# Shared operations offered to two engines, and float32 products on both halves of the accumulator

## The chip, the cores and the metric

The kernel runs on one core of a Trainium2 chip. The core has five engines that take their instructions from queues of their own, each in order: TensorE (PE) multiplies matrices and writes PSUM, VectorE (DVE) and ScalarE (ACT) read PSUM and SBUF, GpSimd (POOL) works on SBUF, and SyncE (SP) issues most of the transfers. They wait for each other by semaphores. The metric is the device time of one execution in microseconds (us), the median of several runs.

## The reference

Attention for 4 batches of 8 heads, 768 positions and 64 columns, in which a query sees only the keys of its own hash bucket (six sign bits of a projection), followed by a two-layer network (512 to 2048 to 512 columns, 3072 tokens) with a squared relu:

```python
q_bits = (np.einsum('bhsd,dk->bhsk', q, proj) > 0).astype(np.int64)
k_bits = (np.einsum('bhsd,dk->bhsk', k, proj) > 0).astype(np.int64)
...
mask = q_bucket[:, :, :, None] == k_bucket[:, :, None, :]
scores = scale * np.matmul(q, k.transpose(0, 1, 3, 2))
scores = np.where(mask, scores, -1000000000.0)
...
attn = attn / (np.sum(attn, axis=-1, keepdims=True) + 1e-09)
return np.matmul(attn, v).astype(np.float32)
...
x = np.ascontiguousarray(attn_out.transpose(0, 2, 1, 3)).reshape(B * S, H * D)
...
h = x @ w_in
r = np.maximum(h, 0.0)
g = s * (r * r) + b
return (g @ w_out).astype(np.float32)
```

## The kernel before

One head of one batch is a visit (32 of them); its 768 queries are worked in three chunks of 256, and a visit's chunk is a slot (96 slots). For every slot `weights` computes two score tiles of 128 x 768 on PE (L436, L437), takes the negated row maximum on DVE (L441), the exponential with its row sum on ACT (L442), four small instructions on DVE for the reciprocal (L446 to L449), and scales the weights on POOL (L454). `values` then transposes the weights on PE (L479), four tiles into a PSUM bank at a time, three banks in a slot; copies each bank to SBUF; and multiplies it with the values into the accumulator `av` in PSUM. Between the slots `prep` makes the next visit's operands: transposes (L318), split in a rounded and a rest part on ACT and DVE (L320, L321), the hash (L331 to L333), its comparison (L336), and transfers inside SBUF on SP's queue. Every second head, the result of two heads is split again (L532, L533) and stored to DRAM (`xd`), from where the network's steps (`moe`) load it.

From the ninth visit on (`FULL = 8`) products with the values are made from rounded parts (float32r): a copy of the transposed weights on ACT (L494), the rest on DVE (L495) and two matmuls for each tile, whose rows 0 to 63 and 64 to 127 of `av` are added at the end (L526 on ACT, L528 on DVE). In the first eight visits (batch 0) they are plain float32 matmuls (L503) with 64 output columns, all into partitions 0 to 63 of `av`. Their copies are placed by number: of the three banks of a slot the third goes to DVE (`FD = (2,)`, L487), the others to ACT (L489). The buffers of these visits are float32 tiles which are later exchanged for float32r tiles under the same tag.

The weights of the network arrive as packed 64-bit numbers and are decoded in 32 pieces (`decode`): two conversions on ACT (L274, L275), two bit operations on DVE (L276, L277), an addition on POOL (L278), a cast on ACT (L280) and a subtraction on POOL (L281). `decodes` says how many pieces are in the list by which slot, `PACE = 2` lets two loads be under way. The network's step of 256 tokens can begin once all eight heads of a batch have that chunk, and once its first pieces are decoded: first-layer matmuls L569 to L571, relu, square and scaling on ACT (L575 to L577), the rest part on POOL (L578, L579), second-layer matmuls L590 to L592, a copy on DVE (L597) and the store.

The order of all this is made by a list scheduler (`Plan`) while the kernel is built. Each step has one engine, an estimated duration, a priority and what it reads and writes. The scheduler takes the engine that is free first and gives it the ready step of lowest priority number:

```python
t = max(free.get(e, 0.0), min(ready[i] for i in lst))
...
i = min((i for i in open_[e] if ready[i] <= t + LOOK.get(e, 0.0)), key=lambda i: (self.steps[i][3], i))
```

The result is each engine's fixed order of instructions. Nothing is chosen while the kernel runs.

## Time and profile before

| what | us |
|---|---|
| median of three runs | 1095.4 |
| lowest and highest of them | 1088.42, 1095.47 |
| the profiled execution, its own time | 1091.88 |
| its span, first to last instruction | 1090.1 |
| PE busy in the span | 1062.0 |
| ACT busy | 654.4 |
| DVE busy | 612.9 |
| POOL busy | 502.1 |

The span is that of the profiled execution. In the rows of the profile an instruction is named by its line, engine and operation, with the tile written and the tiles read; a group's row ends with its count, busy time in us, mean duration in ns, and the idle time of the engine just before it with what ended it. A matmul's end is modelled and overlaps the next one's start, so that consecutive records are closer together than their durations say. The chain of waits follows the work back from the last instruction to what released it.

### The profile page before, as it was taken

The numbers are of one execution on the slowest core, as the hardware profiler recorded it, in microseconds if no ns is written. First come the engines' busy times: TensorE is split into PE (matmuls) and PEld (weight loads), VectorE is DVE, ScalarE is ACT, GpSimd is POOL, SyncE is SP. The second block draws the span as 40 slices with busy tenths as digits, with TensorE's granted clock in tenths as the row PEclk, the third lists the DMA queues.
The fourth block names the chain that finished last, engine by engine and source line by source line (L and its number), as shares of the span: only waits on it lengthen the run. The fifth ranks groups of instructions, "written<-read, shape, count | busy, mean of one in ns | idle before, by whom it ended". The sixth has DMA issues, their size and how long they took to land.

```text
span 1090.1 us, 18596 instructions
## 1 busy us (share of the span) xinstructions
PE 1062.0 (97%) x6948; PEld 942.4 (86%) x6948; DVE 612.9 (56%) x1181; ACT 654.4 (60%) x1265; POOL 502.1 (46%) x482
## 2 busy tenths in 40 slices
PE   7999888999999999999999999999999999999998
PEld 6666565898899999999999999999999998898987
DVE  5568886888666667666666766566667520000000
ACT  3567776888566666665666666656657553333332
POOL 2346776888644443444444443444444433333333
PEclk8999998999999999999999999999999999999999
DMA  3347565645322423332332243232323010101000
GB/s 80 83 134 201 160 189 141 160 118 175 80 55 62 121 74 82 94 92 65 92 104 64 74 112 84 54 115 66 83 54 118 3 56 33 58 1 59 17 23 20
DMA packets 85643, 94.14 MB, mean 86 GB/s; under 512 B 52832, under 2 KB 57952, under 8 KB 85552
## 3 DMA queue, kind: packets, MB, share of 16 engines
q1 hardware_dynamic: 80352, 75.90, 26.0%
q10 hardware_dynamic: 5200, 17.05, 5.1%
q8 instruction: 55, 0.90, 0.3%
q14 instruction: 36, 0.29, 0.1%
HBM read 48.24 MB, written 18.87 MB: 62 GB/s over the span
## 4 chain that ended last, share of the span: by engine, by line
PE 71%; issue 13%; POOL 8%; DVE 5%; ACT 2%; POOLq 0%; DVEq 0%; ACTq 0%
PE bank L479 11%; PE bank L436 6%; PE bank L437 6%; PE bank L503 5%; PE bank L569 5%; PE bank L570 5%; PE bank L571 5%; PE bank L590 5%; PE bank L511 5%; PE bank L591 5%; PE bank L592 5%; PE bank L510 4%; POOL glb L579 4%; POOL rb L578 3%; PE bank L318 2%
## 5 line engine op out<-in xcount | busy, mean ns | idle before, releaser
L454 POOL TENSOR_SCALAR eb<-eb,st 128x768 f32<-128x768 f32 x192 | 191.9, 1008 | 217.9 <-DVE st L449 175.2
L569 PE MATMUL bank<-xc,w 128*128 128x256 f32 x768 | 224.5, 292 | 0.0
L441 DVE TENSOR_REDUCE st<-bank 128x1 f32<-128x768 f32 x192 | 182.8, 954 | 73.9 <-PE bank L437 71.4
L570 PE MATMUL bank<-xc,w 128*128 128x256 f32 x768 | 217.0, 283 | 0.0
L571 PE MATMUL bank<-xc,w 128*128 128x256 f32 x768 | 216.9, 282 | 0.0
L442 ACT ACTIVATE eb<-bank,st 128x768 f32<-128x768 f32 x192 | 173.2, 903 | 43.3 <-DVE st L441 36.1
L494 ACT CAST phr<-bank 128x512 fp32r<-128x512 f32 x216 | 125.2, 583 | 123.1 <-PE bank L479 122.0
L578 POOL TENSOR_SCALAR rb<-rb,misc 128x512 f32<-128x512 f32 x96 | 74.8, 779 | 267.0 <-ACT ghb L577 255.7
L495 DVE TENSOR_TENSOR plb<-bank,phr 128x512 fp32r<-128x512 f32 x216 | 147.1, 686 | 80.2 <-ACT phr L494 77.9
L479 PE MATMUL bank<-ident,eb 128*128 128x128 f32 x1152 | 169.0, 276 | 4.4 <-POOL eb L454 2.9
L590 PE MATMUL bank<-w,ghb 128*128 128x512 f32 x384 | 156.5, 407 | 0.0
L592 PE MATMUL bank<-w,glb 128*128 128x512 f32 x384 | 151.4, 394 | 1.9 <-POOL glb L579 1.9
L591 PE MATMUL bank<-w,ghb 128*128 128x512 f32 x384 | 152.6, 398 | 0.0
L479 PEld LDWEIGHTS bank<-ident,eb 128*128 128x128 f32 x1152 | 135.8, 142 | 17.8 <-POOL eb L454 4.8
L569 PEld LDWEIGHTS bank<-xc,w 128*128 128x128 f32 x768 | 146.0, 190 | 4.3 <-issue 0.4
L570 PEld LDWEIGHTS bank<-xc,w 128*128 128x128 f32 x768 | 146.2, 190 | 3.1
L575 ACT ACTIVATE rb<-bank 128x512 f32<-128x512 f32 x96 | 57.5, 598 | 148.1 <-PE bank L571 145.7
L571 PEld LDWEIGHTS bank<-xc,w 128*128 128x128 f32 x768 | 146.0, 190 | 0.0
L436 PE MATMUL bank<-ks,aq 128*128 128x384 f32 x384 | 139.7, 364 | 3.6 <-ACT eb L442 3.5
L437 PE MATMUL bank<-ks,bq 76*128 76x384 f32 x384 | 131.9, 343 | 1.5 <-DVE bq L395 1.5
L579 POOL TENSOR_TENSOR glb<-rb,ghb 128x512 fp32r<-128x512 f32 x96 | 124.2, 1293 | 6.2
L510 PE MATMUL bank<-phr,vsr 128*128 128x256 f32 x432 | 115.1, 288 | 0.0
(88 smaller groups left out, 1723.3 us busy)
## 6 DMA issues: line engine op xcount, KB each, us to landing
xd<-xsb SPq DMA_DIRECT2D x48, 256.0 KB
xc<-xd SPq DMA_DIRECT2D x48, 256.0 KB
ks<-aq SPq DMA_DIRECT2D x30, 384.0 KB
raw<-in_moe_w_in_dram ACTq DMA_DIRECT2D x16, 512.0 KB
raw<-in_moe_w_out_dram ACTq DMA_DIRECT2D x16, 512.0 KB
nat<-in_q_dram SPq DMA_DIRECT2D x32, 192.0 KB
nat<-in_k_dram SPq DMA_DIRECT2D x32, 192.0 KB
ks<-bq SPq DMA_DIRECT2D x30, 192.0 KB
```

Source lines behind the costliest of these rows:

```text
L436: nc.tensor.matmul(o, aq[:, ts], ks[:, 0, cols], start=True, stop=False)
L437: nc.tensor.matmul(o, bq[0:HR, ts], ks[0:HR, 1, cols], start=False, stop=True)
L441: dve(S, lambda a=a, sc=sc: nc.vector.tensor_reduce(nm[:, a:a + 1], sc, AX.XY, ALU.max, negate=True), bk, [nk[a]], pr, 0.95)
L442: act(S, lambda a=a, sc=sc, e=e: nc.scalar.activation(e.rearrange("p (g n) -> p g n", g=2), sc, AF.Exp, bias=nm[:, a:a + 1], accum_out=z[: ...
L454: pool(S, lambda a=a, e=e: nc.gpsimd.tensor_scalar(e, e, rz[:, a:a + 1], u[:, a:a + 1], ALU.mult, ALU.add), [("st", y, 2)], [ek], pr, 1.01)
L479: nc.tensor.transpose(out=bank[:, tb, o:o + P], in_=eb[:, es[a], kt * P:(kt + 1) * P], identity=ident)
L569: nc.tensor.matmul(hp, w[:, 0, fs], xc[:, 0, :], start=(cc == 0), stop=False)
L570: nc.tensor.matmul(hp, w[:, 1, fs], xc[:, 0, :], start=False, stop=False)
L571: nc.tensor.matmul(hp, w[:, 0, fs], xc[:, 1, :], start=False, stop=(cc == NC_ - 1))
L590: nc.tensor.matmul(o, gh[:, ts], w[:, 0], start=(f == 0), stop=False)
L591: nc.tensor.matmul(o, gh[:, ts], w[:, 1], start=False, stop=False)
L592: nc.tensor.matmul(o, gl[:, ts], w[:, 0], start=False, stop=(f == NF - 1))
```

## The change

The scheduler's steps get a list of ways, each with an engine, a duration and the code for it. A step with several ways is offered to each of its engines. An engine passes it over where another would finish it sooner, and the first that takes it keeps it:

```diff
+    def any(self, ways, r=(), w=(), pr=0.0, lag=0.0):
...
-            i = min((i for i in open_[e] if ready[i] <= t + LOOK.get(e, 0.0)), key=lambda i: (self.steps[i][3], i))
+        def best(e, t):
...
+                if len(ways) > 1:
+                    mine = max(t, ready[i]) + next(c for x, c, _ in ways if x == e)
+                    if any(max(free.get(x, 0.0), ready[i]) + c < mine - 1e-9 for x, c, _ in ways if x != e):
+                        continue
...
+    def some(n, fn, r, w, pr, ways):
+        cost = {ACT: 0.095 + n / 1050.0, DVE: (n + 64) / 960.0 + 0.05, POOL: 0.15 + n / 760.0}
+        eng = {ACT: nc.scalar, DVE: nc.vector, POOL: nc.gpsimd}
+        plan.any([(e, cost[e], lambda e=e: fn(eng[e])) for e in ways], r, w, pr)
```

Offered to ACT and DVE are the copies of the transposed weights, the first half of the accumulator's copy, the relu and the output copy; to ACT and POOL the casts of decoded weights and of `xsb`. All of these copies are one line of the changed kernel, L197. The subtraction for `xsb` goes from DVE to POOL in all cases:

```diff
-                if f in FD:
-                    dve(512, lambda: nc.vector.tensor_copy(ph(), src), [("b", tb)], [("ph", y)], pr, 0.65)
-                else:
-                    act(512, lambda: nc.scalar.copy(ph(), src), [("b", tb)], [("ph", y)], pr)
+                copy(512, lambda: ph, lambda: src, [("b", tb)], [("pf", y)], pr, (ACT, DVE))
...
-        act(CH, lambda: nc.scalar.copy(xh, av[0:D]), [("b", 4)], xk, pr)
-        if w >= FULL:
-            dve(CH, lambda: nc.vector.tensor_tensor(xh, xh, av[D:P], ALU.add), [("b", 4)], xk, pr, 0.42)
+        copy(CH, lambda: xh, lambda: av[0:D], [("b", 4)], xk, pr, (ACT, DVE))
+        dve(CH, lambda: nc.vector.tensor_tensor(xh, xh, av[D:P], ALU.add), [("b", 4)], xk, pr, 0.42)
...
-            act(CH, lambda: nc.scalar.copy(xsb[:, 0, :], t), xk, [("xs", 0)], pr)
-            dve(CH, lambda: nc.vector.tensor_tensor(xsb[:, 1, :], t, f32(xsb[:, 0, :]), ALU.subtract), xk + [("xs", 0)], [("xs", 1)], pr, 0.5)
+            copy(CH, lambda: xsb[:, 0, :], lambda: t, xk, [("xs", 0)], pr, (ACT, POOL))
+            pool(CH, lambda: nc.gpsimd.tensor_tensor(xsb[:, 1, :], t, f32(xsb[:, 0, :]), ALU.subtract), xk + [("xs", 0)], [("xs", 1)], pr)
...
-        act(512, lambda: nc.scalar.copy(wt[key][:, 0], g), [gk], [key + (0,)], pr)
+        copy(512, lambda: wt[key][:, 0], lambda: g, [gk], [key + (0,)], pr, (ACT, POOL))
...
-            act(2 * CH, lambda r=r: nc.scalar.activation(r, bank[:, 5, :], AF.Relu), [("b", 5)], [rk], MP)
+            some(2 * CH, lambda e, r=r: e.activation(r, bank[:, 5, :], AF.Relu) if e is nc.scalar else e.tensor_scalar(r, bank[:, 5, :], 0.0, None, ALU.max), [("b", 5)], [rk], MP, (ACT, DVE))
```

The float32 products of the first eight visits alternate. The two tiles of a bank are m = 0 and 1; the first goes to partitions 0 to 63 of `av` and the second to 64 to 127, and the two halves are added at the end as in the later visits. The planner's duration for a pair goes from 0.87 to 0.62 (`FPC`):

```diff
-                        nc.tensor.matmul(av[0:D], VS[x][:, 0, kt], PH[y][:, m], start=(kt == 0), stop=(kt == NT - 1))
-                pe(0.87, mm, [("ph", y)] + vk, [("b", 4)], pr)
+                        nc.tensor.matmul(av[m * D:(m + 1) * D], VF[x][:, kt], PF[y][:, m], start=(f == 0), stop=(f == HT - 1))
+                pe(FPC, mm, [("pf", y), ("vf", x)], [("b", 4)], pr)
```

Their buffers `VF` and `PF` (four in place of three) lie where the last four decoded pieces come later, so that those four loads wait for the eighth visit's end (`held`); the float32r tiles exist from the start. The first two visits' preparation (`prep_still`) works in two halves of 384 columns with transposes of q and k together, half of its key casts are on DVE, and in the new order all of the second visit's preparation stands on DVE ahead of the first reduction. One broadcast transfer to `ks` becomes two. The four small instructions stay on DVE (`SMALL = "dve"`), and `SPLIT = ()` leaves its branches unused. The numbers of the planner change:

```diff
-        return min(ND, int(FIRST * max(0, i - EARLY // 3)) if i < EARLY else 8 + int(RATE * (i - EARLY)))
+        n = int(FIRST * max(0, i - DSTART)) if i < EARLY else int(FIRST * (EARLY - DSTART)) + int(RATE * (i - EARLY))
+        return min(n, ND if i >= H * NCH else ND - 4)
...
-FIRST = 1.2
-RATE = 4.0
+FIRST = 0.8
+RATE = 6.0
 PACE = 2
+DSTART = 3
...
-RATE_DMA = 1.9e5
+RATE_DMA = 2.2e5
...
-FD = (2,)
+FPC = 0.62
```

Three places show what this does to the order. The first is PE near the end of the second visit. `nat` are the next visit's inputs, `eb` the weights that are transposed, `pf` their copies, `vf` the values; the number after a row is how often it stands there in a row. Before:

```order
L503 MATMUL bank<-pf_77,vf_75 64x256 x2
L503 MATMUL bank<-pf_78,vf_75 64x256 x2
L318 MATMUL bank<-ident,nat_66 128x128 x3
L479 MATMUL bank<-ident,eb 128x128 x8
L503 MATMUL bank<-pf_79,vf_75 64x256 x2
L331 MATMUL bank<-aq_68,pjh 64x384
L332 MATMUL bank<-aq_68,pjl 64x384
L333 MATMUL bank<-bq_70,pjh 64x384
L479 MATMUL bank<-ident,eb 128x128 x4
```

And now:

```order
L535 MATMUL bank<-pf_79,vf_76 64x256 x4
L374 MATMUL bank<-aq_68,pjh 64x384
L375 MATMUL bank<-aq_68,pjl 64x384
L376 MATMUL bank<-bq_70,pjh 64x384
L520 MATMUL bank<-ident,eb 128x128 x8
L535 MATMUL bank<-pf_78,vf_76 64x256 x2
L520 MATMUL bank<-ident,eb 128x128 x8
L535 MATMUL bank<-pf_78,vf_76 64x256 x2
L535 MATMUL bank<-pf_79,vf_76 64x256 x4
```

Transposes of two and three banks stand together now, and the products of two banks follow each other; of 144 matmuls before and after, the stretches of one, two and three banks were 26, 11 and 8 and are 27, 12 and 7.

The second is DVE around the first decoded piece (`raw`, `osb`), in the ninth slot. `st` are row statistics, `xpb` the result of two heads, `xsb` its split. Before:

```order
L441 TENSOR_REDUCE st<-bank 128x1
L487 COPY pf_79<-bank 128x512
L533 TENSOR_TENSOR xsb<-xpb,xsb 128x256
L336 TENSOR_SCALAR nat_66<-bank,misc 44x384
L441 TENSOR_REDUCE st<-bank 128x1
L487 COPY pf_79<-bank 128x512
L446 TENSOR_SCALAR st<-st 128x2
L447 TENSOR_SCALAR st<-st 128x2
L448 RECIPROCAL st<-st 128x2
L449 SCALAR_TENSOR_TENSOR st<-st 128x2
L276 TENSOR_SCALAR raw_194<-osb 128x512
L277 SCALAR_TENSOR_TENSOR osb<-osb,raw_194 128x512
```

And now:

```order
L197 COPY pf_78<-bank 128x512
L470 TENSOR_REDUCE st<-bank 128x1
L197 COPY xpb<-bank 64x256
L363 SCALAR_TENSOR_TENSOR bq_70<-bank,misc,aq_68 128x384
L559 TENSOR_TENSOR xpb<-xpb,bank 64x256
L487 TENSOR_SCALAR st<-st 128x2
L488 TENSOR_SCALAR st<-st 128x2
L489 RECIPROCAL st<-st 128x2
L490 SCALAR_TENSOR_TENSOR st<-st 128x2
L318 TENSOR_SCALAR raw_196<-osb 128x512
L379 TENSOR_SCALAR nat_66<-bank,misc 44x384
L319 SCALAR_TENSOR_TENSOR osb<-osb,raw_196 128x512
```

The subtraction for `xsb` has left, the copy of the accumulator's first half (L197, `xpb`) and the addition of its second half (L559) have come.

The third is POOL at the first pieces. `eb` is the scaling of the weights, `w` a decoded weight. Before:

```order
L454 TENSOR_SCALAR eb<-eb,st 128x768 x4
L278 TENSOR_TENSOR osb<-osb,raw_196 128x512
L454 TENSOR_SCALAR eb<-eb,st 128x768 x2
L281 TENSOR_TENSOR w_857<-osb,w_857 128x512
L278 TENSOR_TENSOR osb<-osb,raw_193 128x512
L281 TENSOR_TENSOR w_893<-osb,w_893 128x512
```

And now:

```order
L495 TENSOR_SCALAR eb<-eb,st 128x768 x2
L320 TENSOR_TENSOR osb<-osb,raw_196 128x512
L197 CAST w_688<-osb 128x512
L564 TENSOR_TENSOR xsb<-xpb,xsb 128x256
L323 TENSOR_TENSOR w_688<-osb,w_688 128x512
L320 TENSOR_TENSOR osb<-osb,raw_197 128x512
L495 TENSOR_SCALAR eb<-eb,st 128x768 x2
```

Between the scalings stand now the weight cast that was ACT's and the `xsb` subtraction that was DVE's.

More of the change, by code (lines that the diff above doesn't have):

```diff
@@ L407, in prep_values @@
+        return [lambda i, pr, f=f, g=g: f(g, i, pr) for f in (split, hash_) for g in range(2)]
     def prep_values(w, pr):
@@ L425, in weights @@
         aq, bq, ks = AQ[x], BQ[x], KS[x]
-        nm, z, rz, u = [st[:, y, m] for m in range(4)]
+        nm, z, rz, u, fl = [st[:, y, m] for m in range(5)]
         nk, zk = [[("st", y, m, a) for a in range(TPC)] for m in range(2)]
@@ L470, in tiles @@
         def tiles(f):
-            tb, y = fill_bank(i), nfill[1] % NPH
-            nfill[1] += 1
+            tb, full = fill_bank(i), w < FULL and f not in SPLIT
+            y = nfill[2] % 4 if full else nfill[1] % NPH
+            nfill[2 if full else 1] += 1
             src = bank[:, tb, :]
```

232 lines of the change are left out of this document (127 added, 105 removed).

## The prediction

> **What bounds the kernel now.** I read the page first: the busy shares and the slices of the span.
>
> ```profile
> span 1090.1 us, 18596 instructions
> PE 1062.0 (97%) x6948; PEld 942.4 (86%) x6948; DVE 612.9 (56%) x1181; ACT 654.4 (60%) x1265; POOL 502.1 (46%) x482
> PE   7999888999999999999999999999999999999998
> DVE  5568886888666667666666766566667520000000
> ```
>
> TensorE (PE) is busy for 97% of the span. DVE comes near it only in the first quarter, and that is where PE shows its 8s. So I cut the span into stages and read the windows view: to the last transposes of the third slot (a slot is one head and 256 query rows), to those of the 24th slot, which ends the first batch's attention, then to the 36th, to the end of attention, and to the end. The columns are the length, then the busy time of PE, weight loads, DVE, ACT and POOL, the granted clock, and the DMA share and rate.
>
> ```profile
> core 0: us, PE busy (x) PEld busy (x) DVE busy (x) ACT busy (x) POOL busy (x), PEclk, DMA share, GB/s
> 0.00:41.30 41.30, 34.82 (x174) 26.38 (x175) 23.64 (x64) 16.71 (x31) 11.76 (x18) 0.92 0.21 55
> 41.30:195.60 154.30, 141.90 (x759) 96.98 (x757) 117.35 (x222) 112.55 (x230) 91.88 (x79) 0.98 0.60 166
> 195.60:328.30 132.70, 130.74 (x894) 120.74 (x893) 102.08 (x172) 98.58 (x192) 93.02 (x83) 1.00 0.42 115
> 328.30:880.00 551.70, 549.99 (x3837) 515.49 (x3836) 358.70 (x705) 351.77 (x702) 232.64 (x234) 1.00 0.30 80
> 880.00:1090.10 210.10, 204.55 (x1293) 182.85 (x1291) 11.12 (x19) 74.78 (x112) 72.84 (x71) 1.00 0.10 33
> ```
>
> From 195.6 us on PE is busy for 98.5% and then 99.7% of its stage, so nothing that other engines do there can give much. The second stage is the place: 154.3 us for 21 slots, PE busy 141.9 (92%), DVE 117.4 (76%), ACT 112.6 (73%), POOL 91.9 (60%). The chain of waits and the groups of that stage say what PE does there.
>
> ```profile
> by line: PE bank L503 30.3%; PE bank L479 14.8%; PE bank L436 8.4%; PE bank L437 7.2%; issue 5.8%; DVE st L449 3.1%; DVE st L441 3.0%; PE bank L318 3.0%; DVE raw L276 2.6%; POOL eb L454 2.5%; PE bank L331 2.3%; ACT pf L489 2.2%; DVE pf L487
> L503 PE MATMUL bank<-pf,vf 128*64 128x256 f32 x252 | 64.2, 392 | 5.3 <-ACT pf L489 3.9 <-DVE pf L487 1.2
> ```
>
> The float32 products of the first eight heads (L503) hold 30.3% of the chain and 64.2 of PE's 141.9 us. Most of the rest of the chain is PE too. So in this stage PE is the bound, and these products are its largest item.
>
> **The products.** Before, every product adds into partitions 0 to 63 of the accumulator. The trace has 288 records for the 144 matmuls of the order: each float32 matmul runs as two.
>
> ```profile
> 100.27 1.08 PE L503 MATMUL bank<-pf,vf 128*64 128x256 f32 x4
> 105.85 1.94 PE L503 MATMUL bank<-pf,vf 128*64 128x256 f32 x8
> 45.34 2.80 PE L503 MATMUL bank<-pf,vf 128*64 128x256 f32 x12
> ```
>
> Four records (one pair of products) take 1.08 us, eight 1.94, twelve 2.80: 0.215 us for each record more, and 0.22 for each stretch. After the change the two products of a pair go to partitions 0 to 63 and 64 to 127. If the halves run side by side while records of one half follow each other in order, a stretch of n pairs takes 2n+1 steps of 0.215 where it took 4n: the first record alone, the last alone, each second record of one half beside the first of the other. Over the whole order the changed kernel has 27 stretches of one pair, 12 of two and 7 of three, and saves (27x1 + 12x3 + 7x5) x 0.215 = 98 x 0.215 = 21.1 us of PE, 252/288 of it, 18.4, in the second stage and 2.6 in the first. No trace shows two halves at once, so the bounds are 0 (the row as it is) and 31 (144 steps gone, if no step stood alone); a loss is left out, since the records stay as many and as long. I take 21, since the two records of a matmul are seen in order in the row and nothing in the program ties one half to the other.
>
> The Trainium skill, "TensorEngine Tiling (Array Packing)", section "Key Properties", says that column tiles operate independently, and "TensorE: Matmul & The Clock Gate", Part 3, gives three column tiles a measured 2.38x. By an estimate from that figure (79% of the ideal, so 1.59x for two halves) 62 us of steps would become 39 and the saving would be 23. No run here shows it.
>
> **What the scheduler moves.** With 18.4 less, PE would be busy 123.5 us in the stage, and then DVE is the question. Its rows there, with two of the whole span for work that is new to it:
>
> ```profile
> L441 DVE TENSOR_REDUCE st<-bank 128x1 f32<-128x768 f32 x41 | 38.7, 952 | 16.5 <-PE bank L437 16.3
> L277 DVE SCALAR_TENSOR_TENSOR osb<-osb,raw 128x512 int32<-128x512 int32 x19 | 17.4, 921 | 0.3
> L487 DVE COPY pf<-bank 128x512 f32<-128x512 f32 x21 | 14.4, 685 | 6.2 <-PE bank L479 6.1
> L276 DVE TENSOR_SCALAR raw<-osb 128x512 int32<-128x512 int32 x19 | 11.8, 629 | 0.0
> L449 DVE SCALAR_TENSOR_TENSOR st<-st 128x2 f32<-128x2 f32 x21 | 9.1, 432 | 0.8
> L533 DVE TENSOR_TENSOR xsb<-xpb,xsb 128x256 fp32r<-128x256 f32 x11 | 7.9, 715 | 0.6 <-ACT xsb L532 0.6
> L528 DVE TENSOR_TENSOR xpb<-xpb,bank 64x256 f32<-64x256 f32 x72 | 30.5, 424 | 47.0 <-ACT xpb L526 45.5
> L489 ACT COPY pf<-bank 128x512 f32<-128x512 f32 x42 | 23.8, 585 | 9.2 <-PE bank L479 8.9
> L280 ACT CAST w<-osb 128x512 fp32r<-128x512 f32 x19 | 11.8, 619 | 4.6 <-POOL osb L278 4.4
> L526 ACT COPY xpb<-bank 64x256 f32<-64x256 f32 x21 | 7.6, 363 | 10.2 <-PE bank L503 10.1
> L418 POOL TENSOR_TENSOR vsr<-vn,vsr 128x384 fp32r<-128x384 f32 x24 | 25.3, 1054 | 43.8 <-ACT vsr L417 43.6
> L578 POOL TENSOR_SCALAR rb<-rb,misc 128x512 f32<-128x512 f32 x96 | 74.8, 779 | 267.0 <-ACT ghb L577 255.7 <-PE bank L437 10.9
> ```
>
> I counted the rows of both orders between the sixth and the 48th reduction (slots 4 to 24). On DVE: 22 more additions of the two halves (new L559, priced by L528: 22 x 0.424 = 9.3), 7 more copies of transposed weights (x 0.685 = 4.8), 8 copies of the sum (priced like L528, 3.4), two more decode pairs that come earlier (2 x (0.921 + 0.629) = 3.1), and 10 subtractions for xsb gone to POOL (10 x 0.715 = -7.2). That is +13.4: 130.8 us. ACT loses 8 copies of 0.585, 8 of 0.363, 10 weight casts of 0.619 and a few small ones, 14 us in all: 99. POOL gains 11 subtractions of 256 columns and 11 casts of 512 and 4 of 256. Its own rows bound the two-input kind by 1.05 (L418, 384 columns) from above and the casts by 0.78 (L578, 512 columns); I take 0.8, 0.8 and 0.5, about 20 us: 112. DVE has become the busiest engine, at 131 where PE stood at 142.
>
> The length of the stage is the busy time of its busiest engine over the share that this engine reaches. PE reaches 92% now. DVE reached 95% and 97% in two slices in which it had work waiting:
>
> ```profile
> 120.00:130.00 10.00, 7.93 (x43) 5.13 (x42) 9.47 (x19) 8.38 (x17) 5.53 (x6) 1.00 0.58 170
> 130.00:140.00 10.00, 10.00 (x54) 6.93 (x53) 9.71 (x16) 7.33 (x15) 7.61 (x7) 1.00 0.40 112
> ```
>
> Over the whole stage it has only 76%, waiting for PE most. I take 90%, just under the 92% of today's busiest engine, because DVE's work comes in pieces that wait for three engines: 131/0.90 = 145.5 us, 8.8 less than 154.3. The ends are 100% (131, so -23) and today's 76% (172, so +18).
>
> **The rest.** First stage: the products save 2.6 there. The order now puts all of the second head's preparation on DVE ahead of the first reduction. Before, part of it came later:
>
> ```profile
> 20.70 1.07 DVE L393 TENSOR_SCALAR ks<-bank,misc 12x768 fp32r<-12x768 f32 x1 [1.73 <-PE bank L391]
> 21.78 1.07 DVE L395 TENSOR_SCALAR bq<-bank,misc 12x768 fp32r<-12x768 f32 x1
> ```
>
> So the first softmax starts later and the next two don't stop for these 2.1 us. One half of the key casts moves to DVE as well. I take -1, between -2.6 and +4. The broadcast to ks becomes two transfers, 30 more issues on SP; the preparation of a head runs a whole head (some 22 us) ahead, which hides an issue; without that cover PE's scores would wait for it. Later stages: 11 of 96 relus go to DVE, 18 of 22 output copies to ACT, hidden under a PE that is 98 to 99.7% busy with both engines near 65% of it; 0, within 3 either way. The last four decodes now wait for the buffers of the first eight heads; the order has them at slots 29.5 to 31 (32nd decode before: 32.5), so 0.
>
> **Sum.** -8.8 - 1 + 0 = -9.8 on the profiled execution's 1091.88 us: 1082 us. That execution lies 3.5 us under the median of the three runs (1095.4) and 3.5 over the lowest.
>
> **Rivals.** (A) PE stays the bound: DVE's copies fall into its gaps, PE keeps its 92%, and the stage is 123.5/0.92 = 134. DVE would need 98% of that; with DVE at the 96% of its best slices it is 136.5. That gives -17.8 and -2.6: 1071 us. For it: DVE's idle time is mostly waiting for PE. Against it: that share was never held for long.
>
> (B) The halves don't run side by side. PE keeps 142 in the stage, DVE's 131 fits beside it, and all stays: 1092 us, up to 1097 if DVE held only 82% (131/0.82 = 160). For it: no row shows an overlap.
>
> (C) POOL holds up DVE. DVE's instructions with SBUF operands are stretched where a POOL instruction is in flight:
>
> ```profile
> 100.56 0.16 DVE L449 SCALAR_TENSOR_TENSOR st<-st 128x2 f32<-128x2 f32 x1
> 111.14 0.68 DVE L277 SCALAR_TENSOR_TENSOR osb<-osb,raw 128x512 int32<-128x512 int32 x1
> 111.90 1.30 POOL L278 TENSOR_TENSOR osb<-osb,raw 128x512 int32<-128x512 int32 x1 [1.27 <-DVE st L446]
> 112.14 1.08 DVE L449 SCALAR_TENSOR_TENSOR st<-st 128x2 f32<-128x2 f32 x1
> 113.40 2.40 POOL L454 TENSOR_SCALAR eb<-eb,st 128x768 f32<-128x768 f32 x2 [0.20 <-DVE st L449]
> 113.61 1.33 DVE L277 SCALAR_TENSOR_TENSOR osb<-osb,raw 128x512 int32<-128x512 int32 x1
> 120.90 0.42 DVE L276 TENSOR_SCALAR raw<-osb 128x512 int32<-128x512 int32 x1
> ```
>
> L277 takes 0.68 us alone and 1.33 beside L454; L449 takes 0.16 alone and 1.08 beside L278; L276 alone takes 0.42. The excess in the stage is 19 x (0.921 - 0.68) + 19 x (0.629 - 0.42) + 21 x (0.432 - 0.16) = 14.3 us with POOL busy 60% of the time. With POOL at 112/145 = 77% it grows to 18.3: DVE 135, the stage 150 at 90%, and the time 1086 us. The Trainium skill, "SBUF — State Buffer", section "Who interferes with whom", calls this an exclusive lock, held for the whole instruction; by that rule moving work to POOL speaks against this change, and the rows agree.
>
> (D) Slower: the handoffs, not the load, set DVE's share, so it stays at 76% while the load grows. Each score tile waits on PE and then on DVE:
>
> ```profile
> DVE st L441 <- PE bank L437: 16.3, 14, 2.7
> ACT eb L442 <- DVE st L441: 11.4, 18, 1.5
> ```
>
> The stage becomes 131/0.76 = 172 and the time 1091.9 + 18 - 1 = 1109 us. It turns into a loss of 1% once DVE's share stays under 79% (131/0.79 = 166). Against it: the 16.3 us that DVE waits for scores come from a PE full of products, which shrink.
>
> **Chances.** The forecast 0.42 (its own range 1075 to 1090), A 0.17, B 0.16, C 0.15, D 0.10. About 1% (11 us) is what a measurement can tell from no change here, so faster begins under 1084.4 against the median. Two thirds of the forecast's cases, all of A and a few of C lie there: 0.28 + 0.17 + 0.04 = 0.49. Slower is D alone, 0.10. The rest is 0.41. The range 1068 to 1094 leaves out the far end of A, the upper part of B and D, about 0.18.
>
> **What would show it.** The eight-record stretches of the new L535 at about 1.3 us and the twelves near 1.7, and a group of some 45 us in place of 73 would show the overlap; stretches of 1.94 show B. The last transposes of the 24th slot at 186 us and DVE's busy share near 90% in the stage confirm the middle step; a share under 80% with the same overlap is D, and PE above 90% there is A. L319 well above 0.92 is C. The forecast is wrong as a whole if the time moves after the 24th slot: PE should stay at 98% or more from there to the end of attention.

## The result, and the profile after

The changed kernel takes 1083.6 us (median of 7 runs, 1081.6 to 1085.5) where the kernel before took 1095.3 on the same chip: a ratio of 0.991, 95% interval 0.989 to 0.994. The profiled execution took 1081.91 us, 9.97 less than the 1091.88 of the one before. The seven executions of the kernel before fall into two groups, 1088.4 to 1088.6 and 1095.3 to 1095.6 us, and its profiled one lies between them, so the parts compared below, which are of one execution each, carry some us of chance.

The page of the profiled execution: span, busy time of the engines, then the slices of the span for PE, DVE and the granted clock.

```profile
span 1080.0 us, 18674 instructions
...
PE 1039.1 (96%) x6936; PEld 928.1 (86%) x6936; DVE 654.3 (61%) x1270; ACT 607.2 (56%) x1141; POOL 552.7 (51%) x557
...
PE   6979887999999999999999999999999999999998
...
DVE  6889896988777777768787677667767400000000
...
PEclk7999997999999999999999999999999999999999
```

PE is 23 us less busy than before, but the span is only 10 shorter. In three of the first seven slices PE shows a lower digit than before, DVE has risen to 8s and 9s in five of them, and the clock stands at 7 in two slices where it stood at 8. The windows view, cut at the same events as before (columns: length, busy time of PE, weight loads, DVE, ACT and POOL, granted clock, DMA share and rate):

```profile
0.00:40.10 40.10, 31.19 (x157) 23.36 (x158) 27.95 (x78) 16.81 (x33) 13.62 (x24) 0.83 0.28 65
40.10:190.70 150.60, 126.56 (x770) 84.66 (x768) 127.29 (x245) 101.38 (x202) 112.90 (x106) 0.93 0.62 173
190.70:323.40 132.70, 129.66 (x880) 119.96 (x879) 109.06 (x187) 89.42 (x169) 96.39 (x89) 0.99 0.40 111
323.40:855.30 531.90, 531.90 (x3747) 501.50 (x3746) 387.40 (x756) 316.19 (x613) 248.97 (x263) 1.00 0.31 83
855.30:1080.00 224.70, 219.76 (x1393) 198.60 (x1391) 2.63 (x6) 83.44 (x125) 80.83 (x79) 1.00 0.09 30
```

| part | before | after | difference | forecast |
|---|---|---|---|---|
| first stage | 41.3 | 40.1 | -1.2 | -1 |
| second stage | 154.3 | 150.6 | -3.7 | -8.8 |
| from the 24th slot to the end | 894.5 | 889.3 | -5.2 | 0 |

The sum is the forecast one (-10.1 for -9.8), its parts are not. In the second stage PE fell from 141.9 to 126.6 us, but its share fell from 92% to 84%; DVE, at 127.3, has 84.5%. So neither engine fills the stage. The products themselves did more than was forecast. PE's timeline (start, length, line, shapes, records):

```profile
41.55 0.65 PE L535 MATMUL bank<-pf,vf 128*64 128x256 f32 x4
...
44.48 1.51 PE L535 MATMUL bank<-pf,vf 128*64 128x256 f32 x12
...
60.95 1.08 PE L535 MATMUL bank<-pf,vf 128*64 128x256 f32 x8
```

Four, eight and twelve records take 0.65, 1.08 and 1.51 us where they took 1.08, 1.94 and 2.80: 0.43 for four records more in place of 0.86, exactly half. What PE waits for in the second stage has changed too. The waits view of the changed kernel there (waiting instruction, what it waits for, total us, times, longest):

```profile
PEld bank L520 <- POOL eb L495: 21.0, 24, 2.2
POOL eb L495 <- DVE st L490: 20.3, 13, 4.5
ACT pf L197 <- PE bank L520: 19.5, 17, 2.0
PE bank L520 <- POOL eb L495: 14.7, 20, 2.1
```

And the row of the kernel before for the same wait, of the weight loads of the transposes on POOL's scaling:

```profile
PEld bank L479 <- POOL eb L454: 4.6, 7, 1.3
```

The transposes now wait for POOL's scaling of the exponentials: the weight loads 21.0 us in place of 4.6, the matmuls 14.7 (the two overlap, and aren't added; PE's idle time in the stage is 150.6 - 126.6 = 24.0 us). In the chain of waits of that stage the scaling, 2.5% before, now has 8.6%:

```profile
by line: PE bank L520 10.6%; issue 9.6%; POOL eb L495 8.6%; PE bank L535 7.4%; DVE st L470 6.9%; POOL w L323 5.3%; PE bank L465 5.2%; DVE pf L197 4.5%; PE bank L466 4.3%; DVE raw L318 4.0%; DVE osb L319 3.9%; DVE st L487 3.8%; DMA ks<-bq 3.
```

The last thing to see is the clock. The windows view of the changed kernel, around two of the times at which the granted clock fell:

```profile
75.98:79.39 3.41, 1.13 (x6) 0.79 (x6) 2.53 (x4) 2.39 (x6) 3.27 (x4) 1.00 0.98 251
79.39:82.81 3.42, 3.42 (x11) 2.80 (x10) 2.33 (x7) 2.15 (x5) 2.36 (x3) 0.50 0.76 237
...
164.72:168.14 3.42, 0.93 (x6) 0.74 (x7) 3.27 (x5) 1.04 (x4) 3.42 (x3) 1.00 1.00 242
168.14:181.79 13.65, 11.95 (x46) 7.36 (x46) 6.25 (x13) 8.96 (x17) 10.40 (x10) 0.50 0.45 117
```

PE was busy 1.13 of 3.41 us (33%), and the next 3.42 ran at half the clock; it was busy 0.93 (27%), and the next 13.65 us, four times 3.41, ran at half. Call (1 - granted clock) x length the lost clock: 0.07 x 150.6 = 10.5 us in the second stage, where it was 0.02 x 154.3 = 3.1 before. The Trainium skill, "TensorE: Matmul & The Clock Gate", Part 1, describes such a gate, with a free-running window of 3413 ns and half rate after an idle one; the length agrees with these rows, but here a window that was a third busy was enough.

Two questions are open, then: which engine or chain the second stage follows, if not PE's or DVE's load, and what each half of the change (the alternation, and the choice of engines with the rest) gave.

### The profile page after: what moved, and what is told of

The parts are those of the page before. It is cut to its first block, busy times and chain, and to the rows that moved or that the text cites. A ratio compares the mean times of both kernels' runs of the same rounds, so it can differ in the third digit from the quotient of the medians.

```text
span 1080.0 us, 18674 instructions
## 1 busy us (share of the span) xinstructions
PE 1039.1 (96%) x6936; PEld 928.1 (86%) x6936; DVE 654.3 (61%) x1270; ACT 607.2 (56%) x1141; POOL 552.7 (51%) x557
## 4 chain that ended last, share of the span: by engine, by line
PE 65%; issue 15%; POOL 10%; DVE 8%; DMA 1%; ACT 1%; POOLq 0%; SPq 0%; ACTq 0%; DVEq 0%
PE bank L520 10%; PE bank L465 5%; PE bank L466 5%; PE bank L600 5%; PE bank L601 5%; PE bank L602 5%; PE bank L623 5%; PE bank L543 5%; PE bank L621 5%; PE bank L622 5%; PE bank L542 5%; POOL glb L610 4%; POOL rb L609 3%; DVE st L470 2%; POOL eb L495 1%
## 5 line engine op out<-in xcount | busy, mean ns | idle before, releaser
L495 POOL TENSOR_SCALAR eb<-eb,st 128x768 f32<-128x768 f32 x192 | 194.6, 1021 | 203.2 <-DVE st L490 147.2
L600 PE MATMUL bank<-xc,w 128*128 128x256 f32 x768 | 222.6, 290 | 0.0
L520 PE MATMUL bank<-ident,eb 128*128 128x128 f32 x1152 | 171.9, 279 | 15.7 <-POOL eb L495 15.3
L527 DVE TENSOR_TENSOR plb<-bank,ph 128x512 fp32r<-128x512 f32 x216 | 145.6, 685 | 29.0 <-ACT ph L197 26.7
L600 PEld LDWEIGHTS bank<-xc,w 128*128 128x128 f32 x768 | 147.1, 192 | 3.5
L465 PE MATMUL bank<-ks,aq 128*128 128x384 f32 x384 | 142.4, 371 | 7.8 <-ACT eb L471 7.8
L606 ACT ACTIVATE rb<-bank 128x512 f32<-128x512 f32 x85 | 50.8, 598 | 160.4 <-PE bank L602 153.5
L197 ACT CAST ph<-bank 128x512 fp32r<-128x512 f32 x134 | 77.6, 585 | 105.4 <-PE bank L520 97.7
```

The lines of the kernel that those rows point to most:

```text
L465: nc.tensor.matmul(o, aq[:, ts], ks[0][:, cols], start=True, stop=False)
L495: pool(S, lambda a=a, e=e: nc.gpsimd.tensor_scalar(e, e, rz[:, a:a + 1], u[:, a:a + 1], ALU.mult, ALU.add), [("st", y, 2), ("st", y, 3)], ...
L520: nc.tensor.transpose(out=bank[:, tb, o:o + P], in_=eb[:, es[a], kt * P:(kt + 1) * P], identity=ident)
L600: nc.tensor.matmul(hp, w[:, 0, fs], xc[:, 0, :], start=(cc == 0), stop=False)
```

## The experiments

Twelve kernels ran, in three groups, each beside the kernel before on one chip. Times are medians; ratios are against the kernel before, which took 1095.8, 1095.4 and 1091.2 us in the three groups. The changed kernel was not run again in these groups; its own 1081.6 to 1085.5 us are what a run's times are set beside, since the kernel before varies by 4 to 8 us within a group. Stage lengths come from the profiled execution, between the last transposes of the third and the 24th slot.

How far one execution can be trusted shows in the kernel with the network's shared operations put back (below). Every engine's order in it is the changed kernel's until behind the second stage, so it is a second draw of that stage:

```profile
41.36:193.88 152.52, 127.95 (x769) 85.91 (x768) 126.66 (x249) 101.36 (x202) 112.67 (x107) 0.93 0.62 171
```

It took 152.5 us for 150.6, so differences of 2 us in this stage say nothing. Behind the 24th slot, the changed kernel and the five kernels below in which all of its order stays took 887.7 to 889.6 us.

### The alternation alone undone

```diff
-  nc.tensor.matmul(av[m * D:(m + 1) * D], VF[x][:, kt], PF[y][:, m], start=(f == 0), stop=(f == HT - 1))
+  nc.tensor.matmul(av[0:D], VF[x][:, kt], PF[y][:, m], start=(kt == 0), stop=(kt == NT - 1))
```

> The changed kernel in its own order, but both products of a pair add into partitions 0 to 63 again; partitions 64 to 127 of the accumulator are set to zero once at the start, so the addition of the two halves stays and adds zero. Everything else, order and engines, is as in the changed kernel. Theory 1 (the overlap of the halves carries the gain of the second stage, and without it TensorE is the bound again): the eight-record stretches take 1.94 us again in place of 1.08, TensorE is busy 25 us longer in the second stage (126.6 to about 151), its share is 92% or more, the stage takes 160 to 165 us in place of 150.6 and the whole 1092 to 1098. Theory 2 (the handoffs between engines set the stage, and TensorE's time only fills gaps that are there anyway): TensorE's lost 42 us take up the 25, the stage grows by 5 us at most and the whole stays under 1088.

1096.6 us, ratio 1.002 (1.000 to 1.003). The second stage in the windows view:

```profile
44.09:205.57 161.48, 146.67 (x770) 99.55 (x768) 126.88 (x245) 101.86 (x202) 110.92 (x106) 0.97 0.59 162
```

The same stretches of products, in PE's timeline:

```profile
45.53 1.08 PE L536 MATMUL bank<-pf,vf 128*64 128x256 f32 x4
...
48.87 2.80 PE L536 MATMUL bank<-pf,vf 128*64 128x256 f32 x12
...
62.34 1.94 PE L536 MATMUL bank<-pf,vf 128*64 128x256 f32 x8
```

Theory 1: the stretches take 1.08, 1.94 and 2.80 us again, PE is busy 20 us longer (25 were expected), at 91% of its stage, and the stage takes 161.5 us. But of those 20 us only 10.9 came out at the end: PE idles 14.8 us in this stage in place of 24.0, so the other half had been given back in waits. Behind the 24th slot 889.6 us remain, as in the changed kernel, so the alternation has no part in what was gained there.

### The alternation alone, in the kernel before

```diff
-  nc.tensor.matmul(av[0:D], VS[x][:, 0, kt], PH[y][:, m], start=(kt == 0), stop=(kt == NT - 1))
-  pe(0.87, mm, ...)
+  nc.tensor.matmul(av[m * D:(m + 1) * D], VS[x][:, 0, kt], PH[y][:, m], start=(f == 0), stop=(f == HT - 1))
+  pe(0.62, mm, ...)
-  if w >= FULL:
-      dve(CH, lambda: nc.vector.tensor_tensor(xh, xh, av[D:P], ALU.add), ...)
+  dve(CH, lambda: nc.vector.tensor_tensor(xh, xh, av[D:P], ALU.add), ...)
```

> The kernel before with the alternation alone: a pair's products go to the two halves, a stretch is priced 0.62 in place of 0.87 in the planner, and the two halves are added in the first eight heads too. All operations keep the engines that they had. Theory 1 (the alternation makes the gain of the first two stages, the engine choice and the rest of the change that of the later stages): eight-record stretches at 1.08, second stage about 150 (154.3 before), last transposes of the 24th slot near 190, 894 us from there to the end as before, in all 1086 to 1088. Theory 2 (without the engine choice DVE or ACT take over as the bound): DVE is busy 127 us and more with the new additions, at the 76% of before the stage takes 165 us and the time is 1100. Theory 3 (the engine choice costs the second stage more through POOL than it gives): the stage takes 143 to 147, in all 1080 to 1084.

1096.0 us (1091.8 to 1104.5), ratio 1.003 (1.000 to 1.006): nothing gained. The second stage:

```profile
36.73:196.12 159.39, 129.12 (x772) 86.95 (x771) 127.23 (x247) 113.46 (x230) 90.84 (x79) 0.93 0.58 159
```

PE is 12.8 us less busy than before and the stage is 5.1 us longer. Theory 1 falls. Theory 2 has the direction, not the size: DVE took 127.2 us as it said, at 80% and not at 76%. The clock stands at 0.93, as in the changed kernel: 11.2 us of lost clock. So the alternation alone loses 5.1 us in the second stage and 3.0 behind it (897.5 from the 24th slot on), against 4.6 won in the first (36.7), and everything else without the alternation (the run before, in the order made for it) gives nothing either. The gain needs the two together.

### The engine choice alone undone

```diff
-  copy(512, ... [("pf", y)], pr, (ACT, DVE))
+  copy(512, ... [("pf", y)], pr, (DVE,) if f == 2 else (ACT,))
-  copy(512, lambda: wt[key][:, 0], ..., pr, (ACT, POOL))
+  copy(512, lambda: wt[key][:, 0], ..., pr, (ACT,))
-  pool(CH, lambda: nc.gpsimd.tensor_tensor(xsb[:, 1, :], t, f32(xsb[:, 0, :]), ALU.subtract), ...)
+  dve(CH, lambda: nc.vector.tensor_tensor(xsb[:, 1, :], t, f32(xsb[:, 0, :]), ALU.subtract), ..., 0.5)
...
```

> The changed kernel, with every shared operation that the kernel before had too put back on the engine it had there (transposed weights on ACT with the third on DVE, sums of products, weight casts, xsb casts and relus on ACT, the subtraction for xsb and the output copies on DVE). The alternation and all else stay. Theory 1 (POOL's longer work holds up TensorE: of the changed kernel's waits in the second stage the largest are behind POOL): POOL falls from 113 to about 92 us there, the waits of TensorE behind L495 from 36 to under 10 us, the stage to 144 to 147 us and the whole to 1076 to 1079. Theory 2 (the choice spreads the load, and that is what the stage lives on): the stage takes 154 us or more, the whole 1086 or more. If the later stages give their 5 us back (894 from the 24th slot on in place of 889), those 5 come from the choice; if they stay at 889, from another part of the change.

1090.7 us, ratio 0.996 (0.994 to 0.999). The second stage in the windows view:

```profile
41.85:199.91 158.06, 132.03 (x779) 90.90 (x778) 124.27 (x245) 113.41 (x231) 91.28 (x80) 0.89 0.60 166
```

Theory 2. POOL fell to 91 us as theory 1 had it, and the stage grew by 7.5 us all the same. Lost clock is 17.4 us here, the most of all runs. The ten executions lie between 1082.7 and 1094.5 us and the profiled one, at 1093.6, near their upper end, so the 7.5 us are more than the typical loss. The median is 7.1 us over the changed kernel's. Behind the 24th slot it takes 891.9 us, 2.6 of the 5.2 us back.

### Only POOL's new work put back

```diff
-  copy(512, lambda: wt[key][:, 0], ..., pr, (ACT, POOL))
+  copy(512, lambda: wt[key][:, 0], ..., pr, (ACT,))
-  copy(CH, lambda: xsb[:, 0, :], ..., pr, (ACT, POOL))
-  pool(CH, ... ALU.subtract), ...)
+  copy(CH, lambda: xsb[:, 0, :], ..., pr, (ACT,))
+  dve(CH, ... ALU.subtract), ..., 0.5)
```

> The changed kernel with only the work that POOL had gained put back: weight casts and xsb casts on ACT, the subtraction for xsb on DVE. The choice between ACT and DVE stays. Theory 1 (POOL's handoffs hold the second stage): POOL falls from 113 to about 92 us there, the waits of TensorE behind L495 from 36 to under 10, the stage to 143 to 147 and the whole to 1075 to 1079. Theory 2 (POOL's waits are only the last of several chains of the same length, since the scores cannot start before exponentials, sums and mask of the slot ahead are done): the waits move to ACT and DVE, the stage stays within 2 us of 150.6 and the whole within 2 of 1082. Theory 3 (DVE is the bound): its busy time grows by the seven or more subtractions, 5 us at 0.7 each, and the stage grows by as much, to 155.

1096.8 us, ratio 1.003 (1.001 to 1.006). The second stage in the windows view:

```profile
41.22:200.52 159.30, 131.15 (x769) 86.91 (x768) 137.46 (x262) 107.33 (x215) 95.13 (x80) 0.91 0.58 161
```

And in the waits view:

```profile
POOL eb L495 <- DVE st L490: 29.4, 17, 4.8
PEld bank L520 <- POOL eb L495: 19.3, 19, 3.9
```

POOL lost 17.8 us of work, and PE waits for L495 nearly as long as before (19.3 of 21.0), since L495 itself now waits 29.4 us for DVE in place of 20.3. Of the three theories the third is nearest, with a larger loss than it said (8.7 us for 10.2 us more on DVE). The order differs from the changed kernel's here, so this run alone doesn't say that DVE's load is what costs; the two runs that follow, with the order left as it is, do better.

### Less work for DVE, in the same order

```diff
+  z = 1 if w < FULL else CH
...
-  dve(CH, lambda: nc.vector.tensor_tensor(xh, xh, av[D:P], ALU.add), [("b", 4)], xk, pr, 0.42)
+  dve(CH, lambda: nc.vector.tensor_tensor(xh[:, :z], xh[:, :z], av[D:P, :z], ALU.add), [("b", 4)], xk, pr, 0.42)
```

> The changed kernel in its own order, but the new addition of the two halves covers one column in place of 256 in the first eight heads, so their output is not the sum. DVE is about 22 x 0.3 = 6 to 8 us less busy in the second stage, nothing else changes. Theory 1 (the prediction's middle step: DVE is the bound, and the stage is its busy time over a share that it keeps): at 84.5% the stage falls by 7 to 9 us, to 142 to 144, the whole to 1073 to 1076. Theory 2 (a chain over several engines sets the stage, in which DVE has slack): DVE's share falls to 80% and the stage by 3 us at most.

1083.3 us, ratio 0.993 (0.989 to 0.996). The second stage in the windows view:

```profile
40.76:191.39 150.63, 126.61 (x769) 85.50 (x768) 124.20 (x248) 101.40 (x202) 113.29 (x106) 0.93 0.62 173
```

The group of the shortened addition in that stage (busy time and mean ns behind the bar):

```profile
L560 DVE TENSOR_TENSOR xpb<-xpb,bank 64x1 f32<-64x1 f32 x21 | 3.3, 158 | 0.7
```

The additions fell from 8.9 to 3.3 us; DVE's total fell by 3.1, half of what was expected, since other DVE instructions took longer (L319 0.955 us in place of 0.878). The stage did not move: 150.63 for 150.60. Theory 2. A stage of DVE's busy time over a fixed share would have lost 3.1/0.845 = 3.7 us, against 2 us of chance; the run speaks against the prediction's middle step, and the next one does so more strongly. It says nothing of DVE's instructions between scores and scaling, for which POOL waits 20.3 us.

### Less work for POOL on the way to the transposes, in the same order

```diff
-  pool(S, lambda a=a, e=e: nc.gpsimd.tensor_scalar(e, e, ...
+  pool(S, lambda a=a, e=e: nc.gpsimd.tensor_scalar(e[:, :HS] if w < FULL else e, e[:, :HS] if w < FULL else e, ...
```

> The changed kernel in its own order, but POOL's scaling of the exponentials (L495) covers 384 of the 768 columns in the first eight heads, so the other half stays unscaled. POOL is about 42 x 0.5 = 21 us less busy in the second stage, and each tile of exponentials is ready some 0.5 us sooner. Theory 1 (POOL holds the stage, being the last link ahead of the transposes): TensorE's waits behind L495 fall from 36 us to under 15 and the stage by 8 us or more. Theory 2 (DVE is the bound): the stage falls by 4 us at most, and what it falls by comes from DVE instructions that are stretched less beside POOL (DVE's busy time 123 or less in place of 127).

1075.5 us, ratio 0.985 (0.981 to 0.990). The second stage in the windows view:

```profile
43.87:185.41 141.54, 123.67 (x769) 82.55 (x768) 127.29 (x249) 101.00 (x202) 98.34 (x106) 0.96 0.66 185
```

The group of the scalings in that stage:

```profile
L495 POOL TENSOR_SCALAR eb<-eb,st 128x384 f32<-128x384 f32 x41 | 31.1, 767 | 27.1 <-DVE st L490 21.7 <-ACT pf L197 2.6 <-PE bank L376 1.4
```

And the waits of the transposes for them:

```profile
PEld bank L520 <- POOL eb L495: 9.6, 15, 1.7
...
PE bank L520 <- POOL eb L495: 5.8, 11, 1.4
```

41 scalings take 31.1 us in place of 45.7, and the stage is 9.1 us shorter. (The first stage took 43.9 us here for 40.1, so the 24th slot ends 5.3 us earlier; the whole is 8.1 us under the changed kernel.) DVE is as busy as before, to the hundredth (127.29), and its share is now 127.29/141.54 = 90%. The waits behind L495 fell from 21.0 and 14.7 to 9.6 and 5.8 us. Lost clock fell too, from 10.5 to 5.7 us; at the price found below (3.5 us for 10.5) that is some 1.6 of the 9.1 (an estimate). Theory 1: the stage follows a chain that runs through POOL's scaling, not the load of DVE. POOL itself, at 75% before this edit, was not full either.

### Transposes added in front of the slots' transposes

```diff
   def tr():
+      for n in range(8 if full and f == 0 else 0):
+          nc.tensor.transpose(out=bank[:, tb, n % 4 * P:(n % 4 + 1) * P], in_=ident, identity=ident)
       for m in range(2):
```

> The changed kernel, its order and engines as they are, with work added to TensorE and none taken away: in the first eight heads, eight more transposes of the constant identity matrix run in front of the first transposes of each slot, into the accumulator bank that those then overwrite (nothing reads them). TensorE waits there for L495, about 1.5 us a slot; eight transposes take 8 x 0.109 = 0.9 us. Theory 1 (gaps cost TensorE twice: after a stretch of 3.41 us in which it was busy less than about 55%, the trace shows the granted clock at 0.50 for 3.41 us or a multiple, 10.5 us of lost clock in the second stage): with the gaps filled the clock stays at 1.00 over nearly all of the second stage, lost clock under 4 us, TensorE busy 15 to 21 us longer there, and the stage is shorter, 143 to 148 in place of 150.6, the whole 1074 to 1079. Theory 2 (TensorE's half rate falls into time that DVE sets anyway): the clock rises as in theory 1, but the stage stays within 2 us of 150.6 and the whole within 2 of 1082. Theory 3 (the added transposes stand in the way of others): the stage grows by 5 us or more, up to 21.

1087.1 us, ratio 0.993 (0.991 to 0.995). The second stage in the windows view:

```profile
42.11:199.20 157.09, 141.68 (x938) 104.52 (x936) 126.46 (x245) 101.92 (x202) 113.71 (x106) 0.93 0.60 166
```

A piece of PE's timeline (in brackets the idle time ahead, and what ended it):

```profile
171.82 0.93 PE L518 MATMUL bank<-ident 128*128 128x128 f32 x7
173.57 0.33 PE L522 MATMUL bank<-ident,eb 128*128 128x128 f32 x1 [0.82 <-POOL eb L495]
175.95 0.90 PE L522 MATMUL bank<-ident,eb 128*128 128x128 f32 x3 [2.06 <-POOL eb L495]
```

Theory 3, and no test of the other two: the clock stayed at 0.93. The long gaps lie elsewhere, as the timeline shows: not ahead of a slot's first transpose but behind it, where the second tile of exponentials is missing (2.06 us), and ahead of score products. The filling stood in the way in 21 slots and missed the places that matter.

### Transposes added in the long gaps

```diff
+  def busy(kind):
+      k = made[kind] = made.get(kind, -1) + 1
+      for _ in range(BUSY.get((kind, k), 0)):
+          nc.tensor.transpose(out=bank[:, 4, 384:512], in_=ident, identity=ident)
...
+  BUSY = {('score', 4): 14, ('score', 8): 3, ('score', 40): 14, ('hash', 8): 8, ('turn', 252): 12, ('turn', 253): 14, ('score', 94): 7}
```

> The changed kernel, its order and engines as they are, with 72 transposes of the identity matrix added for TensorE just where its long gaps stand, written to a corner of the accumulator's memory that nothing uses, so that they wait for nothing: 17 in the first stage ahead of the score products that wait 3.63 and 0.86 us, 55 in the second stage (ahead of the waits at 76.3, 119.0, 163.5, 165.5 and 176.5 us). Theory 1 (the half rate after a gap costs time): the drops of the clock behind these five places go, the second stage's lost clock falls from 10.5 us to under 4 and the stage gets shorter by 3 to 7 us, the first stage by 1 to 4; the whole 1073 to 1079. Theory 2 (the half rate falls into time that other engines set): the clock comes up all the same, and the second stage stays within 2 us of 150.6.

1080.9 us, ratio 0.990 (0.986 to 0.994). The second stage in the windows view:

```profile
41.86:188.95 147.09, 124.99 (x824) 85.32 (x823) 127.53 (x245) 101.45 (x202) 112.74 (x106) 1.00 0.65 178
```

PE's timeline at the gap that stood at 76.3 us:

```profile
77.85 0.34 PE L474 MATMUL bank<-ks,bq 76*128 76x384 f32 x1
78.03 1.69 PE L345 MATMUL bank<-ident 128*128 128x128 f32 x14
80.52 0.44 PE L473 MATMUL bank<-ks,aq 128*128 128x384 f32 x1 [0.80 <-ACT eb L479]
```

Theory 1. 55 instructions more in the second stage, and it is 3.5 us shorter, with the clock at 1.00 throughout. PE's total busy time is even lower (124.99 for 126.56), with nothing at half rate. So in these two executions 10.5 us of lost clock cost 3.5 us of time, to within the 2 us of chance. The first stage did not gain (41.9 us); over the kernels whose order is the same up to there it lies between 40.1 and 44.1 us. The whole, 1080.9 us (1080.2 to 1081.5), is 2.7 us under the changed kernel, and not in the 1073 to 1079 of the theory.

### The network's shared operations, the old decode pace

```diff
-  some(2 * CH, ... [rk], MP, (ACT, DVE))
+  some(2 * CH, ... [rk], MP, (ACT,))
-  copy(512, ... [("os", t)], MP, (DVE, ACT))
+  copy(512, ... [("os", t)], MP, (DVE,))
```

> The changed kernel with the network's two shared operations put back: all relus on ACT, all output copies on DVE. Theory 1 (these two give the 5 us by which the time from the last transposes of the 24th slot to the end shrank): that time goes from 889 back to 893 or 894, the whole to 1086. Theory 2 (they come from the copies of the transposed weights, that ACT and DVE now share in attention): it stays at 889 within 1.5, the whole within 2 of 1082.

1086.1 us, ratio 0.993 (0.990 to 0.995), with 890.0 us behind the 24th slot: that is 0.7 us of the 5.2, next to a spread of 1.9 us for one and the same order. For this part it is theory 2's number, though nothing here shows that the copies of the transposed weights gave the 5.2. The rest of the loss lies in the first two stages, where the order is the changed kernel's (41.4 and 152.5 us), and is chance.

```diff
-  n = int(FIRST * max(0, i - DSTART)) if i < EARLY else int(FIRST * (EARLY - DSTART)) + int(RATE * (i - EARLY))
+  n = int(FIRST * max(0, i - EARLY // 3)) if i < EARLY else 8 + int(RATE * (i - EARLY))
-  FIRST = 0.8
-  RATE = 6.0
+  FIRST = 1.2
+  RATE = 4.0
```

> The changed kernel with the pace at which the kernel before decoded the network's weights: none before the eighth slot, then 1.2 a slot, and few around the 21st to 24th slot, in place of 0.8 a slot from the fourth and six a slot from the 21st. Theory 1 (the earlier and denser decodes, their transfers and their work on DVE and POOL, stretch the second stage, above all slots 21 to 24): DVE's busy time falls by 3 us or more there and the stage by as much, to 147 or less, with the same time or up to 2 us more behind it; the whole 1077 to 1080. Theory 2 (what is taken from the stage comes back, since the network waits for its weights): the stage is shorter, but from the 24th slot to the end TensorE loses as much; the whole within 2 of 1082 or above it.

1087.9 us, ratio 0.994 (0.992 to 0.997). The second stage takes 151.5 us with DVE at 132.5, and 892.9 remain behind it. Neither theory: DVE had more to do in the stage, not less, and with 87% of it DVE was busier than in the changed kernel in nearly the same time. With the old pace, and the other order that comes with it, the time behind the 24th slot is 3.6 us longer.

### Other prices for the planner

```diff
-FPC = 0.62
+FPC = 0.45
```

> The changed kernel with one number of the planner changed: a pair of float32 products is priced 0.45 us, which is what the trace shows for two steps of 0.215, in place of 0.62. Theory 1 (the order suffers from the wrong price): TensorE's lost time in the second stage falls, the stage is 3 us or more shorter, the whole 1076 to 1079. Theory 2 (the price hardly moves the order, since DVE is what the stage waits for): the whole within 3 of 1082.

1079.1 us (1077.1 to 1080.3), ratio 0.986 (0.984 to 0.989): the fastest of the kernels that leave nothing out. The second stage in the windows view:

```profile
40.68:183.59 142.91, 125.13 (x761) 81.35 (x760) 122.80 (x242) 102.64 (x207) 97.89 (x94) 0.96 0.66 179
```

And its longest wait:

```profile
PEld bank L520 <- POOL eb L495: 13.5, 19, 2.0
```

Theory 1: the stage is 7.7 us shorter. POOL has 15 us less to do in it (fewer casts and decodes, which came later), the transposes' loads wait 13.5 us for L495 in place of 21.0, and lost clock is 5.7. Some of it comes back: 891.8 us behind the 24th slot, 2.5 more.

```diff
-  dve(1, inverse, nk + zk, [("st", y, 2), ("st", y, 3)], pr, 0.55)
+  dve(1, inverse, nk + zk, [("st", y, 2), ("st", y, 3)], pr, 0.9)
...
```

> As the run with 0.45 us for a pair of products, and three more prices of the planner set to what the trace shows: the group of small operations after a softmax 0.9 in place of 0.55, the two decode operations of DVE 0.60 and 0.92 in place of 0.54 and 0.88. Theory 1 (a price nearer to the trace gives a better order): 1075 or less. Theory 2 (the order reacts to such numbers without a direction; the 4 us of the last run are one draw): anything from 1075 to 1086, without a gain over 1079.

1085.6 us, ratio 0.995 (0.992 to 0.998), with a second stage of 152.8 and 895.1 behind it in the profiled execution, which with 1089.8 us is one of the longer of ten (1081.4 to 1091.2). Theory 2. Even the shortest is 1.1 us over the longest of the run above: three more prices nearer to the trace took the gain away, so that gain can't be put down to a better price as such; what it shows is what a stage with fewer waits for POOL looks like.

## Why the prediction was right, and where it was not

The time, 1082 against a measured 1083.6, is right; of the working, half is, and that the sum came out is luck.

**The products: right in kind, too small.** The step "a stretch of n pairs takes 2n+1 steps" failed in size: stretches take 2n steps, since records of the two halves start together (6 to 7 ns apart in the trace) from the first. In the second stage L535 is busy 38.8 us where L503 was 64.2: 25.4 us saved, not 18.4. The upper bound, with no step standing alone, was the value to take. Rival B is out. The estimate from the 2.38x of the Trainium skill, "TensorE: Matmul & The Clock Gate", Part 3 (a saving of 23 over the whole order) was nearer than the row's reading, and low too.

**The scheduler's moves: right, a little too large for DVE.** DVE 127.3 for a forecast of 130.8 (9.9 us more than before, not 13.4), ACT 101.4 for 99, POOL 112.9 for 112.

**The length of the stage: the step that failed.** "The length of the stage is the busy time of its busiest engine over the share that this engine reaches", with DVE at 90%, gave -8.8; it measured -3.7. DVE's share was 84.5%. The last transposes of the 24th slot ended at 190.7 us and not at the 186 that would have confirmed the step. The fault is not that number but the rule: 3.1 us taken from DVE moved the stage by 0.0 (with 2 us of chance), while 14.6 us taken from POOL's scaling moved it by 9.1 and 20 us given to PE by 10.9. After the change no engine was over 85% busy, and the stage followed a chain that passes from the scores over DVE, ACT, DVE and POOL to the transposes; that POOL's link holds it is shown, the links before it are read from the waits alone. The words "waits for three engines" stood in the prediction, as a reason for a share; they were the mechanism.

**POOL: seen in the wrong place.** Rival C had POOL stretch DVE's instructions, by the exclusive lock of the Trainium skill, "SBUF — State Buffer", section "Who interferes with whom". L277 had taken 0.921 us; as L319 it took 0.878 with POOL busy 75% of the stage in place of 60%. The cost was not there: PE's weight loads waited 21.0 us for POOL's scaling in the second stage. Nor could the new work simply be taken off POOL: the run that did so, in another order, lost 13 us.

**The clock: left out.** The row of the second stage had a granted clock of 0.98 before, and I made nothing of it. A PE with less to do has gaps, and the three drops of the clock in this stage lie behind gaps of 2.28 us, 1.12 us, and 1.69 and 2.05 us together: 10.5 us of lost clock, about 3.5 us of time, as the filled gaps showed. Of the 10.5, 3.1 were there before; if each costs the same, 7.4/10.5 x 3.5 = 2.5 us are new, half of the 5.1 by which the stage missed its forecast (an estimate).

**The start: -1.2 for -1**, which the spread of 40.1 to 44.1 us in one and the same order makes no confirmation.

**The later stages: -5.2 for 0.** The prediction said it would be wrong as a whole if the time moved after the 24th slot, and it moved. The windows view of that part, first the kernel before:

```profile
195.60:1090.10 894.50, 885.27 (x6020) 819.08 (x6018) 471.90 (x896) 525.13 (x1005) 398.49 (x386) 1.00 0.27 74
```

and the changed one:

```profile
190.70:1080.00 889.30, 881.32 (x6014) 820.06 (x6012) 499.08 (x949) 489.05 (x907) 426.19 (x429) 1.00 0.27 74
```

PE is busy 4.0 us less for six records fewer (six of 0.147 us, 0.9), and idle 1.2 us less. The largest single item is the network's L569, now L600: 220.8 us for 762 records in place of 223.5 for 765. Why PE's busy time fell isn't shown. "Hidden under a PE that is 98 to 99.7% busy" took a busy PE for one that can't get shorter. Undoing the alternation changes nothing there (889.6), undoing the network's shared operations 0.7, which is no difference, all engine choices 2.6, POOL's part of them alone 3.9, the decode pace 3.6. These don't add up to 5.2, since each makes another order. Which of them did it is not settled.

So two errors of 5 us cancelled: the stage fell 5.1 us less than forecast, and the part behind it 5.2 more. Rival D came closest to a true warning: in the kernel before with the alternation alone DVE had 80% and the stage did grow, by 5.1 us.

## What to carry to other kernels

When the bound engine of a stage is relieved and the next one is at 85%, don't divide its load by a share: follow the chain from tile to tile, and ask which instruction on it has to be shorter or earlier. Look at the granted clock of each stage before taking work away from TensorE; where gaps of 2 us are left, some useless matmuls in just those gaps can pay. And test a change of two parts as two: here neither the alternation alone (1096.0 us) nor everything else without it (1096.6) was worth anything. One changed price of the planner won 4 us, and three more lost 6 again, so an order is to be measured and not trusted for its prices.

## What the hardware showed that I had not expected

Float32 matmuls whose outputs lie in partitions 0 to 63 and 64 to 127 run fully side by side, two records (starting 6 to 7 ns apart) to a step of 0.215 us, from the first record of a stretch to the last: 0.65, 1.08 and 1.51 us for 4, 8 and 12 records, where one half alone takes 1.08, 1.94 and 2.80.

The granted clock falls in a grid. In the changed kernel's trace the four drops after the start, at 79.39, 120.35, 168.14 and 226.17 us, lie 12, 14 and 17 times 3.413 us apart, and each lasts one window or four. Cut all fourteen traces into windows of 3.413 us on that grid and take PE's busy time in each: after the first 30 us, each of the 32 windows at full clock with PE busy less than 49% was followed by half rate; between 49 and 65% it went either way, and above that never. (Where the grid lies is known from the drops; moved by 0.04 us, the 49% becomes 48 to 51%.) Once at half rate, PE had to be busy for nearly all of a window, 89% at least, to get the full clock back, and sometimes more was not enough.

That grid lies differently in each trace: counted from the first instruction, its windows begin at 0.89 us in the changed kernel, at 1.65 in the one with less DVE work and at 0.02 in the one with less POOL work, whose orders are the same. So a gap can fall into one window in one execution and across two in another, which may be why times differ from run to run. That is not shown; the runs show that the time follows the mean clock. The kernel before took 1088.6 to 1088.9 us in the four of 31 runs with a mean clock of 0.997 and 1095.8 to 1096.4 in those with 0.988; the kernel with three more prices took 1081.4 to 1081.8 at 0.991 and 1087.8 to 1091.2 at 0.981 to 0.983.
